# TensorE on zeros before the first keys, the second chunk's keys and queries loaded earlier, and the late relus, sums and stores rearranged, in a linear-attention and Fourier-mixing kernel

## The chip, the core and the metric

The kernel runs on one core of a Trainium2 chip. The core has five instruction queues that run side by side, each in its own program order, and wait for each other by semaphores: TensorE (matrix products; PE in the profile, with its weight loads as PEld), VectorE (DVE), ScalarE (ACT), GpSimd (POOL) and SyncE (SP), which here only issues DMA transfers. The metric is the device time of one execution in microseconds, lower is better.

## What is computed

Two blocks in a row. The first is a linear attention with decay, in 64-row blocks; the second takes its output as `x`, mixes it by a Fourier transform over sequence and width, normalises, and applies a two-layer network.

```python
# attention, per block of 64 rows (B=4, H=8, S=768, D=64)
intra = einsum(einsum(qb, kb) * Dmask, vb)
inter = einsum(qb * lam_pow, kv_state)
out[:, :, sl] = intra + inter
kv_state = lam_block * kv_state + einsum(kb * rev_pow, vb)

# x is (4, 768, 512)
mixed = real(fft(fft(x, axis=1), axis=2))
u = x + mixed
un = (u - mean(u)) / sqrt(var(u) + 1e-6)
out = u + maximum(un @ w_ch1, 0) @ w_ch2       # 512 -> 2048 -> 512
```

## The kernel before

Everything is float32. A float32 product shows in the profile as two TensorE records, a transpose (a product with an identity) as one.

**Front end.** `attn(b)` runs over six chunks of 128 rows of batch `b`. `attn_in(b, c)` issues three loads on SP's queue, `k`, `q` and `v` of the chunk (line 303, 256 KB each, from a pool of two buffers a name), makes the decayed keys `kd` on GpSimd (310), transposes keys (314) and queries (319) on TensorE and copies them out on ScalarE as `kT` (316) and `qT` (321). `attn_out` makes the scores (338), multiplies them by the decay on VectorE into `sc` (343), updates the state (358; 360 copies it for the first chunk, 362 and 363 add to it later), forms the output (373, 379), copies it out on ScalarE as `oT` (382) and turns it (395). Beside the attention of batch 0, `weights()` brings in the weights: each piece is a 512 KB load `raw` on SP (214), two ScalarE steps (225, 228) and five VectorE steps (226, 230, 232, 234, 235), because the weights come as 64-bit floats and are put together as float32 on the chip. The decay tables come from `lam` by scans on VectorE (161, 168).

The planner is a tile scheduler: it gives each instruction a place in its engine's queue by due times, except where the code pins the program order (`tc.keep_in_program_order`). The generators' `yield` values only set how pieces of work are woven.

**Middle.** The Fourier mixing (`fft_ln`) and the first four groups of the network (`mlp`, lines 749 and 763) are woven with the attention of the later batches.

**Late part.** Eight groups of 256 rows, in four pairs, go through the network by a seven-product scheme (Strassen-Winograd: sums of quarter matrices, seven products for eight). `late()` runs `first_layer(0)` for the first pair, and then `second_layer` and `deep_pair` for the others, in which each product is again split in seven (`seven`, lines 1124 and 1198). Of each of these products the seven parts are read out of PSUM by ScalarE (a first part) or VectorE (the others; 1206 in the second layer).

In `first_layer` block `i` of eight makes seven products of four TensorE records each, all on line 1031, in three PSUM banks X, Y and Z. This document names a product by its two factors (the names given to `prod`):

- `begin(i)`: X = a11·b11, copied out by ScalarE (1052); Y = a12·b21, added on VectorE (1054) and put through the relu there (1055); `begin` runs up to three blocks ahead.
- then X += s2·t2, copied out as `a12` (ScalarE, 1069); Z = s3·t3; X += s1·t1, copied out as `a22` (ScalarE, 1072); `a22` += Z (VectorE, 1073) and its relu (1074).
- `finish(i)`, one block later: X += s4·b22, whose relu goes out as `a21` (ScalarE, 1041, tile `sv` in the profile); Z += a22·t4; `a12` += Z (VectorE, 1043) and its relu (VectorE, 1044); `s1` = a21 + a22 (1045) and `s3` = a11 − a21 (1046).

A product that adds to a bank cannot start until the copy out of that bank before it is done: s1·t1 of a block waits for the copy 1069, s4·b22 for the copy 1072, a22·t4 for the addition 1073. In the profile the tiles `a11`, `a12`, `a22` are `ha`, and `s1`, `s3` are `hs`. Meanwhile GpSimd makes the sums of the second layer's weights (`keep_sums`, lines 855 and 859), four operations of 128x512 for each of seven products.

`inputs(j)` builds the sums of a later pair's input; its first step is the subtraction on line 941, pinned in VectorE's program order, which needs the tile `ur` loaded on line 894.

`store` (734) writes the result: rows of the lower half of a batch by SP (736), those of the upper half by an indirect DMA from GpSimd (738), whose rows come from an index table. `out_low` and `out_high` are two views of the output that the scheduler takes to be disjoint; two writes to the same view wait for each other. The last pair stores two upper tiles and two lower ones, the lower ones in pieces.

Of the kernel before, what the change touches and what calls it, by code (L numbers as in the profile page):

```python
# [11 lines left out]
F32 = mybir.dt.float32  # L12
# [4 lines left out]
AF = mybir.ActivationFunctionType  # L17
ALU = mybir.AluOpType
# [59 lines left out]
def kernel(  # L78
# [10 lines left out]
    nc = tc.nc  # L89
    B, H, S, D = q.shape  # L90
    DM = H * D
    DFF = moe_w_ch1.shape[1]
    C = 128
# [6 lines left out]
    HM = DM // 2  # L100
# [15 lines left out]
    def front_pool(name, bufs):  # L116
        return front_end.enter_context(tc.tile_pool(name=name, bufs=bufs, side="left"))
# [4 lines left out]
    const = front_pool("const", 1)  # L122
    ld = front_pool("ld", 2)
# [16 lines left out]
    def new(pool, shape, tag, **kw):  # L140
        cnt[0] += 1
        return pool.tile(shape, F32, tag=tag, name=f"{tag}{cnt[0]}", **kw)

    def psum_a(shape):
        return new(pa, shape, "pa")

    def psum_m(shape):
        return new(pm, shape, "pm")

    lamb = const.tile([128, H], F32, name="lamb")
    nc.scalar.dma_start(lamb, lam.rearrange("(o h) -> o h", o=1).broadcast_to([128, H]))
    ident = const.tile([128, 128], F32, name="ident")
# [30 lines left out]
    def row_of(j, n=128):  # L186
        return bass.IndirectOffsetOnAxis(ap=ix[0:n, j:j + 1], axis=0)
# [9 lines left out]
    def load_tables(i):  # L197
        if i == 1:
            nc.sync.dma_start(cs, cn["cs"].ap())
            nc.sync.dma_start(ix, cn["ix"].ap())  # L200
        elif i == 2:
            nc.sync.dma_start(dt, cn["dt"].ap())
# [80 lines left out]
    def pair(t, hp):  # L283
        return t[:, 2 * hp:2 * hp + 2, :].rearrange("p a d -> p (a d)")
# [6 lines left out]
            head = attn_in(b, c + 1) if c < NC - 1 else attn_in(b + 1, 0) if b in LEADS else ()  # L291
            yield from attn_out(b, c, head)

    ins, oTs, eo = {}, {}, {}
    LEADS = (0,)
    TURNED = (0,)
    first = const.tile([128, HP, 1], F32, name="first")

    def attn_in(b, c):
        rows = slice(c * C, (c + 1) * C)  # L300
        kt, qt, vt = (new(ld, [C, H, D], nm) for nm in ("k", "q", "v"))
        for t, src in ((kt, k), (qt, q), (vt, v)):
            nc.sync.dma_start(t, src[b, :, rows, :].rearrange("h p d -> p h d"))
        if b == 0:
            load_tables(c)

        kd = None
        if c < NC - 1:
            kd = new(at, [C, H, D], "kd")
            nc.gpsimd.tensor_tensor(kd, kt, kpow, op=ALU.mult)  # L310

        ptk = psum_a([128, HP, C])
        for hp in range(HP):
            nc.tensor.transpose(ptk[:, hp, :], pair(kt, hp), ident)  # L314
        kT = new(at, [128, HP, C], "kT")
        nc.scalar.copy(kT, ptk)
        ptq = psum_a([128, HP, C])
        for hp in range(HP):
            nc.tensor.transpose(ptq[:, hp, :], pair(qt, hp), ident)  # L319
        qT = new(at, [128, HP, C], "qT")  # L320
        nc.scalar.copy(qT, ptq)  # L321
        qs = None
        if c > 0:
            qs = new(at, [128, HP, C], "qs")
            nc.vector.tensor_tensor(qs, ptq, qpow, op=ALU.mult)
        ins[b, c] = kT, qT, qs, kd, vt
        yield 1.2

    def attn_out(b, c, head):
        kT, qT, qs, kd, vt = ins.pop((b, c))  # L330
# [9 lines left out]
        for hi in range(2):  # L340
            t = new(at, [C, HP, C], "sc", bufs=3)
# [11 lines left out]
        if not last:  # L353
            pu = psum_a([128, HP, D])
            for hp in range(HP):
                for hi in range(2):
                    h = 2 * hp + hi
                    mm(pu[HD[hi], hp, :], lhsT=kd[:, h, :], rhs=vt[:, h, :], start=True, stop=True)  # L358
            if c == 0:
                nc.vector.tensor_copy(s_new, pu)  # L360
            else:
                nc.gpsimd.tensor_tensor(s_new, s_old, spow.broadcast_to([128, HP, D]), op=ALU.mult)
                grown = nc.vector.tensor_tensor(s_new, s_new, pu, op=ALU.add)
            if not padded:
                yield 0.9
# [11 lines left out]
        for hp in range(HP):  # L377
            for hi in (1, 0) if padded else (0, 1):
                mm(po[HD[hi], hp, :], lhsT=vt[:, 2 * hp + hi, :], rhs=sc[hi][:, hp, :],  # L379
                   start=(c == 0 and hp == 0), stop=(hp == HP - 1), skip_group_check=True)  # L380
# [78 lines left out]

    uts, utd, ud, held = {}, {}, {}, {}  # L460
    ys = [const.tile([128, 2 * NK], F32, name=f"ys{i}") for i in range(5)]
    odd = const.tile([128, HM], F32, name="bs")
    for t in ys + [odd]:
        nc.gpsimd.memset(t, 0.0)

    gather = nc.gpsimd.indirect_dma_start
# [261 lines left out]
    ORDER = [(b, g) for b in range(B) for g in (1, 2, 0)]  # L728
    PLAIN, LATE = ORDER[:4], ORDER[4:]

    out_low, out_high = dram_disjoint_views(out.rearrange("b s d -> (b s) d"), 2)

    def store(b, T, y, cols=slice(0, DM)):
        if T < HC:
            row = S * b + 128 * T
            nc.sync.dma_start(out_low[row:row + 128, cols], y[:, cols])
        else:
            nc.gpsimd.indirect_dma_start(out=out_high,
                                         out_offset=row_of(2 + HC * (b + 1) + T - HC),
                                         in_=y[:, :], in_offset=None)  # L740

# [67 lines left out]
    V = nc.vector  # L809
# [108 lines left out]
    def inputs(j):  # L918

        P, r = pairs[j], s2.u.pop(j)  # L920
        b11, b21, b12, b22 = r[:, 0, 0:2], r[:, 0, 2:4], r[:, 1, 0:2], r[:, 1, 2:4]

        def sx(shape):
            return new(s2.hp, shape, "sx", bufs=6)

        P.U = U = dict(b11=b11, b21=b21, b22=b22, t3=b12)
        if j < DEEP:
            U["t1"], U["t2"], U["t4"] = t1, t2, t4 = [sx([128, 2, G * 128]) for _ in range(3)]
            V.tensor_tensor(t1, b12, b11, op=SUB)
            yield 0.0  # L930
            V.tensor_tensor(t2, b22, t1, op=SUB)
            yield 0.0
            V.tensor_tensor(t4, b21, t2, op=SUB)
            yield 0.0
            V.tensor_tensor(b12, b22, b12, op=SUB)
            yield 0.0
            return


        B11, B12, B21, B22 = (r[:, :, k::2, m:m + 128] for k in range(2) for m in (0, 128))  # L940
        tc.keep_in_program_order(V.tensor_tensor(B12, B22, B12, op=SUB))
        yield 0.0
        t1 = U["t1"] = sx([128, 2, G * 128])
        V.tensor_tensor(t1, b12, b11, op=SUB)
        yield 0.0
        V.tensor_tensor(b12, b22, b12, op=SUB)
        yield 0.0
        T2, T1, T4 = [sx([128, 2, 2, 128]) for _ in range(3)]
        V.tensor_tensor(T2, B12, B11, op=ADD)
        yield 0.0  # L950
        V.tensor_tensor(T1, B22, T2, op=SUB)
        yield 0.0
        V.tensor_tensor(T4, B21, T2, op=SUB)
        yield 0.0
        P.T = {n: [t[:, h, k] for t in (T1, T2, T4)]
               for n, h, k in (("b11", 0, 0), ("b21", 0, 1), ("t3", 1, 0), ("b22", 1, 1))}
        t2, t4 = U["t2"], U["t4"] = [sx([128, 2, G * 128]) for _ in range(2)]
        V.tensor_tensor(t2, b22, t1, op=SUB)
        yield 0.0
        q2, q1, q4 = [new(s2.hp, [128, 3, 128], "sv", bufs=3) for _ in range(3)]  # L960
        for i, n in enumerate(("t2", "t1", "t4")):
            C11, C12, C21, C22 = (U[n][:, k, m:m + 128] for k in range(2) for m in (0, 128))
            if n == "t4":
                nc.gpsimd.tensor_tensor(t4, b21, t2, op=SUB)
                yield 0.0
            nc.gpsimd.tensor_tensor(q2[:, i], C12, C11, op=ADD)
            nc.gpsimd.tensor_tensor(q1[:, i], C22, q2[:, i], op=SUB)
            nc.gpsimd.tensor_tensor(q4[:, i], C21, q2[:, i], op=SUB)
            P.T[n] = [q1[:, i], q2[:, i], q4[:, i]]
            yield 0.0  # L970
# [53 lines left out]
    def first_layer(j):  # L1024

        P = pairs[j]
        h, U = P.h, P.U

        def prod(ps, a, b, i, first):
            for kt in range(2):  # L1030
                nc.tensor.matmul(ps, lhsT=s2.A[a][:, kt, 128 * i:128 * i + 128], rhs=U[b][:, kt, :],  # L1031
                                 start=(first and kt == 0), stop=(kt == 1), skip_group_check=True)

        def two(t):
            return t.rearrange("p (s k) -> p s k", s=G)

        def finish(i, X, Z):
            a11, a12, a22, s1, s3 = (h[n][:, :, i, :] for n in ("a11", "a12", "a22", "s1", "s3"))
            prod(X, "s4", "b22", i, False)
            a21 = new(s2.hp, [128, G, 128], "sv", bufs=3)  # L1040
            nc.scalar.activation(a21, two(X), AF.Relu)
            prod(Z, "a22", "t4", i, False)
            V.tensor_tensor(a12, two(Z), a12, op=ADD)
            V.tensor_scalar(a12, a12, 0.0, None, op0=ALU.max)
            V.tensor_tensor(s1, a21, a22, op=ADD)
            V.tensor_tensor(s3, a11, a21, op=SUB)

# [13 lines left out]
        for i in range(HF):  # L1061
            a12, a22 = (h[n][:, :, i, :] for n in ("a12", "a22"))
# [375 lines left out]
```

## Time and profile before

| | us |
|---|---|
| median of 3 runs | 777.26 (775.27 to 777.77) |
| the profiled execution | 773.78 |
| its span | 771.7 |
| TensorE busy (5784 records) | 752.6, 98% of the span |
| VectorE busy | 602.8, 78% |
| ScalarE busy | 231.1, 30% |
| GpSimd busy | 178.4, 23% |

The span runs from the first instruction to the last that the profiler sees. A timeline line gives start, duration, engine, line of the kernel, operation, output tile and inputs, shapes and count; in square brackets stands the time that the engine sat idle before it and what ended that. The profile shows a granted clock of 1.00 in every slice. TensorE starts its first product at 5.05 us; after that it is idle for some 14 us in all, of which 1.6 us lie in three waits after 100 us, and 4.8 us at the very end.

### The profile page before, as it was taken

The page shows a single profiled execution, that of the slowest core. Times are in us where ns is not written, and L with a number is a line of the kernel's source. Part 1 is how long each engine was busy: PE and PEld are TensorE (multiplying, and loading weights), DVE is VectorE, ACT ScalarE, POOL GpSimd, SP SyncE. Part 2 cuts the span into 40 slices and gives each one's busy share as a digit, 9 for nine tenths or more (in the row PEclk, how much of TensorE's full clock was granted, in tenths as well). Part 3 has the DMA queues.
Part 4 walks back from the last instruction along what each step waited for, and adds up shares of the span by engine and source line. Part 5 has one row for each costly group of instructions (what it writes and reads, how often), then busy time and mean ns, then how long its engine had stood idle before and what let it go on. Part 6 is the DMA issues. An engine that isn't in the chain of part 4 may idle for free.

```text
span 771.7 us, 15006 instructions
## 1 busy us (share of the span) xinstructions
PE 752.6 (98%) x5784; PEld 646.7 (84%) x5784; DVE 602.8 (78%) x1167; ACT 231.1 (30%) x532; POOL 178.4 (23%) x202
## 2 busy tenths in 40 slices
PE   6989999999999999999999999999999999999997
PEld 5777877777685967769747899999999999999997
DVE  6999998784936575336898999788986699758984
ACT  3755443435521221322101221034301341024310
POOL 3223330021111113220105941360015001230013
PEclk9999999999999999999999999999999999999999
DMA  9979732347943149731433465876545456455442
GB/s 240 274 161 250 195 125 86 106 96 181 246 117 94 45 82 270 176 97 35 113 65 124 150 218 164 273 234 202 180 124 178 125 186 182 127 175 180 144 141 70
DMA packets 154924, 120.22 MB, mean 156 GB/s; under 512 B 114286, under 2 KB 116974, under 8 KB 154854
## 3 DMA queue, kind: packets, MB, share of 16 engines
q1 hardware_dynamic: 147792, 100.51, 46.7%
q0 software_dynamic: 4032, 12.99, 4.7%
q10 hardware_dynamic: 3030, 5.78, 2.1%
q8 instruction: 46, 0.75, 0.4%
q14 instruction: 24, 0.20, 0.1%
HBM read 88.04 MB, written 31.20 MB: 155 GB/s over the span
## 4 chain that ended last, share of the span: by engine, by line
PE 88%; DVE 7%; DMA 2%; ACT 1%; issue 1%; POOL 0%; SPq 0%; DVEq 0%; ACTq 0%
PE p L1198 22%; PE p L1124 17%; PE pm L763 13%; PE pm L749 13%; PE p L1031 6%; PE pa L603 3%; PE pa L379 3%; PE pa L338 3%; PE pa L373 2%; PE pa L314 1%; PE pa L358 1%; PE pa L395 1%; DVE sc L343 1%; PE pa L763 1%; PE pa L319 1%
## 5 line engine op out<-in xcount | busy, mean ns | idle before, releaser
L749 PE MATMUL pm<-ut,w 128*128 128x256 f32 x512 | 118.3, 381 | 0.0
L763 PE MATMUL pm<-w,hr 128*128 128x512 f32 x240 | 108.7, 596 | 0.1
L749 PEld LDWEIGHTS pm<-ut,w 128*128 128x128 f32 x512 | 94.7, 190 | 14.4 <-issue 2.7
L763 PEld LDWEIGHTS pm<-w,hr 128*128 128x128 f32 x240 | 43.8, 190 | 45.5 <-issue 43.8
L1219 POOL TENSOR_TENSOR y<-y,u 128x512 f32<-128x512 f32 x12 | 19.9, 1661 | 186.8 <-DVE y L1228 155.5
L1198 PE MATMUL p<-tx,sx 128*128 128x128 f32 x400 | 52.7, 275 | 0.0
L1198 PEld LDWEIGHTS p<-tx,sx 128*128 128x128 f32 x400 | 48.6, 192 | 0.0
L1133 DVE TENSOR_TENSOR ha<-p,ha 128x512 f32<-128x512 f32 x60 | 40.1, 686 | 8.6 <-PE p L1124 8.6
L1204 ACT COPY y<-p 128x128 f32<-128x128 f32 x48 | 12.8, 266 | 103.6 <-PE p L1198 103.1
L310 POOL TENSOR_TENSOR kd<-k,decay 128x512 f32<-128x512 f32 x20 | 21.7, 1083 | 86.5 <-PE pa L358 50.1
L343 DVE TENSOR_TENSOR sc<-pa,decay 128x512 f32<-128x512 f32 x48 | 30.9, 683 | 11.7 <-PE pa L338 11.5
L1206 DVE TENSOR_TENSOR y<-p,y 128x128 f32<-128x128 f32 x92 | 25.6, 285 | 15.6 <-PE p L1198 9.1
L1198 PE MATMUL p<-w,ha 128*128 128x128 f32 x288 | 37.4, 275 | 0.0
L1133 DVE TENSOR_TENSOR hs<-p,hs 128x512 f32<-128x512 f32 x39 | 26.2, 685 | 12.4 <-PE p L1124 12.4
L338 PEld LDWEIGHTS pa<-qT,kT 64*128 64x128 f32 x384 | 25.1, 193 | 12.2 <-ACT qT L321 6.4
L1198 PEld LDWEIGHTS p<-w,ha 128*128 128x128 f32 x288 | 34.9, 192 | 0.1
L638 POOL TENSOR_SCALAR ve<-mv 128x2 f32<-128x2 f32 x12 | 6.2, 519 | 120.0 <-DVE mv L635 120.0
L757 ACT ACTIVATE hr<-pm 128x256 f32<-128x256 f32 x44 | 16.7, 382 | 57.6 <-PE pm L749 53.7
L1124 PE MATMUL p<-sx,tx 128*128 128x128 f32 x264 | 33.9, 275 | 0.0
L338 PE MATMUL pa<-qT,kT 64*128 64x128 f32 x384 | 30.1, 292 | 2.9 <-ACT qT L321 2.9
L1124 PEld LDWEIGHTS p<-sx,tx 128*128 128x128 f32 x264 | 31.7, 192 | 0.0
L379 PE MATMUL pa<-sc,v 128*64 128x128 f32 x384 | 28.9, 282 | 1.3 <-DVE sc L343 1.0
(274 smaller groups left out, 1748.4 us busy)
## 6 DMA issues: line engine op xcount, KB each, us to landing
tx<-td SPq DMA_DIRECT2D x84, 256.0 KB, 2.9
raw<-in_moe_w_ch_dram SPq DMA_DIRECT2D x32, 512.0 KB, 4.3
tx<-sd SPq DMA_DIRECT2D x63, 256.0 KB, 2.8
k<-in_k_dram SPq DMA_DIRECT2D x24, 256.0 KB, 3.7
q<-in_q_dram SPq DMA_DIRECT2D x24, 256.0 KB, 7.0
v<-in_v_dram SPq DMA_DIRECT2D x24, 256.0 KB, 5.7
td<-tx SPq DMA_DIRECT2D x21, 256.0 KB, 2.0
ud<-x SPq DMA_DIRECT2D x16, 256.0 KB, 3.1
```

Source lines behind the costliest of these rows:

```text
L310: nc.gpsimd.tensor_tensor(kd, kt, kpow, op=ALU.mult)
L338: mm(pss[hi][:, hp, :], lhsT=kT[HD[hi], hp, :], rhs=qT[HD[hi], hp, :], start=True, stop=True)
L343: nc.vector.tensor_tensor(t, pss[hi], decay[:, hi::2, :], op=ALU.mult)
L379: mm(po[HD[hi], hp, :], lhsT=vt[:, 2 * hp + hi, :], rhs=sc[hi][:, hp, :], start=(c == 0 and hp == 0), stop=(hp == HP - 1), skip_group_chec ...
L603: mm = nc.tensor.matmul(ps[:, n, :], lhsT=piece(a, i, n), rhs=cs[0:rows, a, i in (2, 3), n, :], start=(a == 0), stop=(a == 1))
L749: nc.tensor.matmul(ps, lhsT=w1[:, c, 128 * fc:128 * fc + 128], rhs=ut[:, c, :], start=(c == 0), stop=(c == KO - 1))
L763: return nc.tensor.matmul(ps, lhsT=hr[(fc - f0) // 4][:, fc % 4, 128 * i:128 * i + 128], rhs=w2[:, fc, :], start=(fc == f0), stop=(fc == f ...
L1031: nc.tensor.matmul(ps, lhsT=s2.A[a][:, kt, 128 * i:128 * i + 128], rhs=U[b][:, kt, :], start=(first and kt == 0), stop=(kt == 1), skip_gro ...
L1124: nc.tensor.matmul(ps[:, 128 * i:128 * i + 128], lhsT=ab[m][0][:, 128 * i:128 * i + 128], rhs=ab[m][1], start=(start and i == 0), stop=Tru ...
L1133: V.tensor_tensor(o, p, o, op=ADD)
L1198: nc.tensor.matmul(ps[:, 0:HM // 2], lhsT=ab[m][0][i], rhs=ab[m][1][:, i, :], start=(start and i == 0), stop=(i == HF // 2 - 1), skip_grou ...
L1206: V.tensor_tensor(o, ps[:, 0:HM // 2], o, op=ADD)
```

## The change

```diff
--- before.py
+++ after.py
@@ -150,6 +150,18 @@
+    odd = const.tile([128, HM], F32, name="bs")
+    nc.vector.memset(odd, 0.0)
+    nothing = psum_m([128, 128])
+
+    def keep_on(n):
+
+        for _ in range(n):
+            tc.keep_in_program_order(
+                nc.tensor.matmul(nothing, lhsT=odd[:, 0:128], rhs=odd[:, 0:128], start=True, stop=True))
+
+    keep_on(9)
+
     lamb = const.tile([128, H], F32, name="lamb")
@@ -291,16 +303,26 @@
-    ins, oTs, eo = {}, {}, {}
+    ins, oTs, eo, loaded = {}, {}, {}, {}
...
     def attn_in(b, c):
-        rows = slice(c * C, (c + 1) * C)
-        kt, qt, vt = (new(ld, [C, H, D], nm) for nm in ("k", "q", "v"))
-        for t, src in ((kt, k), (qt, q), (vt, v)):
-            nc.sync.dma_start(t, src[b, :, rows, :].rearrange("h p d -> p h d"))
+
+        def load(c, *which):
+            rows = slice(c * C, (c + 1) * C)
+            for nm, src in which:
+                t = loaded[nm, b, c] = new(ld, [C, H, D], nm)
+                nc.sync.dma_start(t, src[b, :, rows, :].rearrange("h p d -> p h d"))
+
+        turned = (("k", k), ("q", q))
+        if ("k", b, c) not in loaded:
+            load(c, *turned)
+        load(c, ("v", v))
+        if (b, c) == (0, 0):
+            load(1, *turned)
+        kt, qt, vt = (loaded.pop((nm, b, c)) for nm in ("k", "q", "v"))
@@ -358,6 +380,8 @@
             if c == 0:
                 nc.vector.tensor_copy(s_new, pu)
+                if b == 0:
+                    keep_on(4)
@@ -459,8 +483,7 @@
-    odd = const.tile([128, HM], F32, name="bs")
-    for t in ys + [odd]:
+    for t in ys:
         nc.gpsimd.memset(t, 0.0)
@@ -728,14 +751,16 @@
-    out_low, out_high = dram_disjoint_views(out.rearrange("b s d -> (b s) d"), 2)
+    out_low, *out_high = dram_disjoint_views(out.rearrange("b s d -> (b s) d"), 3)
+    uppers = [0]
...
         else:
-            nc.gpsimd.indirect_dma_start(out=out_high,
+            uppers[0] += 1
+            nc.gpsimd.indirect_dma_start(out=out_high[uppers[0] % 2],
@@ -938,6 +963,7 @@
+        yield 0.0
         tc.keep_in_program_order(V.tensor_tensor(B12, B22, B12, op=SUB))
@@ -1041,7 +1067,7 @@
             V.tensor_tensor(a12, two(Z), a12, op=ADD)
-            V.tensor_scalar(a12, a12, 0.0, None, op0=ALU.max)
+            nc.scalar.activation(a12, a12, AF.Relu)
             V.tensor_tensor(s1, a21, a22, op=ADD)
```

Five things, by their places:

- Nine products of a 128x128 tile of zeros stand at the head of TensorE's queue, and four more behind the state update of batch 0's first chunk (line 358). Their result is not used. The tile of zeros is `odd`, which was cleared by GpSimd (464) and is now cleared by VectorE as its first instruction.
- On SP's queue `k` and `q` of batch 0's second chunk go out ahead of the first weight piece `raw`, not behind it. `v` of that chunk and all later loads keep their order.
- The relu of `a12` in `first_layer` (line 1044) goes from VectorE to ScalarE.
- In `inputs` the first subtraction (941) comes one step later, so that on VectorE one read of the second layer (1206) goes ahead of it, for each of three pairs.
- The upper stores go by turns through two views, so that each waits for the last but one and not for the one before it.

In the built order of the two kernels nothing else differs but this: the transposes of the second chunk's keys (314) stand on TensorE behind all of the first chunk's 379 and not between them, and the copy of these keys (316) on ScalarE behind `oT` (382) and the first weight piece's 225 and 228.

## The prediction

> **What bounds the kernel now.** I read the page's busy times first, then the chain of waits, then TensorE's own waits, then timelines of the places that the change touches.
>
> ```profile
> PE 752.6 (98%) x5784; PEld 646.7 (84%) x5784; DVE 602.8 (78%) x1167; ACT 231.1 (30%) x532; POOL 178.4 (23%) x202
> PE 88%; DVE 7%; DMA 2%; ACT 1%; issue 1%; POOL 0%; SPq 0%; DVEq 0%; ACTq 0%
> ```
>
> TensorE is the bound. VectorE, ScalarE or a DMA can only cost or give what TensorE waits for them, and those waits are few: 5.1 us for the first keys, some 6 us spread over 15 to 100 us, 0.8 us in `first_layer`, 0.6 us near 499 us, and the tail. So no part can gain much, but a new wait in the late part is lost in full, since TensorE has no idle time behind it in which to catch up.
>
> ```profile
> 5.05 1.08 PE L314 MATMUL pa<-ident,k 128*128 128x128 f32 x4 [5.05 <-DMA k<-in_k_dram]
> 7.96 2.08 PE L338 MATMUL pa<-qT,kT 64*128 64x128 f32 x16 [0.68 <-ACT qT L321]
> 11.45 1.12 PE L314 MATMUL pa<-ident,k 128*128 128x128 f32 x4
> 14.05 0.66 PE L319 MATMUL pa<-ident,q 128*128 128x128 f32 x4
> ```
>
> The start of the timeline: four transposes take 1.08 and 1.12 us until 12.6 us and 0.66 from 14 us on, and the sixteen score records 2.08 us, against 1.16 at 21.48. TensorE runs at about half its speed until some 13 us, 8 us after it begins, though the page's granted clock reads 1.00 throughout.
>
> ```profile
> 424.57 1.13 PE L1031 MATMUL p<-sx,w 128*128 128x256 f32 x4 [0.76 <-DVE ha L1073]
> 430.06 0.38 ACT L1041 ACTIVATE sv<-p 128x256 f32<-128x256 f32 x1 [1.35 <-PE p L1031]
> 431.97 0.37 ACT L1069 COPY ha<-p 128x256 f32<-128x256 f32 x1 [1.52 <-PE p L1031]
> 432.02 0.41 DVE L1045 TENSOR_TENSOR hs<-sv,ha 128x256 f32<-128x256 f32 x1
> 432.36 1.48 DVE L1046 TENSOR_TENSOR hs<-ha,sv 128x256 f32<-128x256 f32 x1
> 432.63 1.03 PE L1031 MATMUL p<-sx,w1s 128*128 128x256 f32 x4
> 433.76 0.41 DVE L1043 TENSOR_TENSOR ha<-p,ha 128x256 f32<-128x256 f32 x1
> 434.21 0.91 DVE L1044 TENSOR_SCALAR ha<-ha 128x256 f32<-128x256 f32 x1
> ```
>
> `first_layer`: VectorE is full, with operations that take 1.48 and 0.91 us while GpSimd works beside it (0.42 and 0.29 for the same after 453.4 us, when GpSimd has done). Block 2's addition 1043 comes at 433.76, while ScalarE has copied block 3's `a12` (1069) at 431.97 and TensorE has gone on with block 3's s1·t1 at 432.63.
>
> **The relus, worked out.** Taken from VectorE: eight times 0.91 us, which TensorE felt as 0.76 us once. Given to ScalarE: eight relus of some 0.40 us (1041, the same size out of PSUM, takes 0.38). ScalarE is idle most of the time here, so the work is free; the wait is not. In the built order ScalarE's queue reads 1041 of block i, the new relu of block i, 1069 of block i+1, 1072 of block i+1. The relu waits for VectorE's 1043 of block i, and behind it queue the two copies that TensorE's next products wait for.
>
> From s4·b22 of block i (435.22 for block 3) to s1·t1 of block i+1 (438.67) TensorE needs 3.45 us. The new path over the same stretch: 1.11 until 1041 starts (436.33), 0.38 for it, then 1045 and 1046, 0.42 for 1043, 0.40 relu, 0.37 copy, four handovers of 0.05: 2.88 us and the two sums. The sums take 0.75 us with GpSimd idle, 1.74 as at 432.02 to 433.76, 2.65 as at 420.18 to 422.83. So s1·t1 comes 0.18, 1.17 or 2.08 us late in each block, at the three speeds.
>
> Block by block: the relus of blocks 0 and 1 stand ahead of 1072. Block 0's 1043 ends at 423.24, so the relu ends at 423.7, block 1's copy at 424.05 instead of 422.50, and s4·b22 starts then, not at 422.79. The old wait of 0.76 us behind it goes, and block 1 leaves 0.4 us late. Block 2: VectorE has shed two relus, but has to wait for 1041 of block 1, which now comes later, and 1043 of block 2 ends at about 434.2 as before; relu to 434.6, copy to 435.0, s1·t1 of block 3 at 435.05 instead of 432.63: 2.4 us late in all. Blocks 3 and 4, with GpSimd still at work: 1.17 each. Blocks 5 and 6, after it: 0.18 each. Together 2.4 + 2.3 + 0.4 = **+5.1 us**. Bounds: if VectorE keeps the 0.9 us it shed, block 3 is 1.5 late, and with free sums 0.18 for each of four more, 2.2; if every block to the fifth meets the slow sums, 2.4 + 3 x 2.08 + 0.2 = 8.8; and if the relu never gates, the old wait goes, -0.8. I take 5.1, since 1.74 is the pitch of four of the six blocks in GpSimd's time.
>
> **The front, worked out.** Added: a clear of 128x256 on VectorE (GpSimd's took 0.30 us), hidden in VectorE's 3.76 us wait for `lam`; the same taken from GpSimd, which waits 3.47 us for the decay anyway. Nine products are 18 records. Eight of the nearest records (1198, 128x128) take 1.06 us with 0.28 for one alone, so 0.11 each, some 0.20 at the slow rate (2.08 to 1.16): 3.6 us, from 1.1 to about 4.8, when the first keys are still landing. A slower rate would push the transposes of 5.05 by 0.2 at most. The four later products, 0.9 us at full rate, stand between 358 and 379, where TensorE would wait for `sc`; at the slow rate they cost up to 1.6 us less that wait.
>
> When does the clock rise? Here it took 8 us from TensorE's first work, with gaps in it. Ends: up when the keys land at 5.05, or 8 us after the zeros begin, at 9.1. I take the middle, 7.0: queries transposed by 7.2, `qT` by 7.8, scores 7.85 to 9.0, `sc` at 9.05 instead of 10.07, state copied by 10.75. VectorE comes to the weight piece (226) next. That piece is late now: on SP's queue two loads, 512 KB, go ahead of it, and at the 250 GB/s of these microseconds that is 2 us; it landed about 8.6 (issued at 3.67, 4.9 to land) and now lands near 11. Behind it queue 226 (0.9), on ScalarE 228 (0.7), `oT` (0.6), 386 (0.2), 225 (0.7), then `kT` and `qT` of chunk 1 (1.2; `kT` was early before, but the scores need both): scores of chunk 1 at 15.3 instead of 15.91, their `sc` at 16.0 instead of 17.10. VectorE is full from there to 70 us and the chain of waits runs through it, so this carries on: **-1.0 us**. With the clock up only at 9.1 the same steps give -0.2. Bounds: -1.8 with the weight piece in time; +0.8 if the zeros do not raise the clock and the four later products run slow in front of 379.
>
> [...]
>
> **The rest.**
>
> ```profile
> 498.54 0.69 DVE L941 TENSOR_TENSOR ur<-ur 128x512 f32<-128x512 f32 x1 [2.70 <-DMA ur<-utd]
> 499.49 1.16 PE L1198 MATMUL p<-w2s,sx 128*128 128x128 f32 x8 [0.57 <-DVE y L1206]
> 765.63 0.97 POOL L738 DMA_INDIRECT out_dram<-y,ix  x1 [2.54 <-DVE y L1206]
> 766.90 0.29 DVE L1206 TENSOR_TENSOR y<-p,y 128x128 f32<-128x128 f32 x1 [0.60 <-PE p L1198]
> ```
>
> The sum 941 waits 2.70 us for its load with a read 1206 queued behind it, and TensorE waits 0.57 us for that read. With the read ahead of the sum this goes: **-0.6**, at worst 0; the other two pairs show no such wait. In the tail the second upper store had its last part from VectorE by 763.6 (a read at 763.32), but issued at 765.63: the first had gone at 762.11 and takes 2.9 to land, 765.0. DVE is named, but had long been done. Without that wait it issues near 763.9 and lands at 766.8. But VectorE's last read is at 766.90, the last SP store goes at 767.2 and lands 1.7 later, 768.9, while the old GpSimd store landed at 768.5: **-0.2**, between 0 and -0.4. The POOL waits of earlier pairs hide behind 50 us of its idle time.
>
> Sum: 5.1 - 1.0 - 0.6 - 0.2 = +3.3 us. The profiled execution took 773.78 (span 771.7 and 2.1 around it), so 777.1 by its clock; it lay 3.5 below the median of the runs, and I add to the median: 777.26 + 3.3 = **780.6 us**.
>
> **Rivals.** A difference under 0.3%, 2.3 us, can't be told from none: 774.9 to 779.6.
>
> Rival 1, the relu gates little: VectorE, rid of 0.9 us in each 5.58, catches up, the sums run at 0.75, and 2.2 us remain of the 5.1. Then 2.2 - 1.8 = +0.4, 777.7. For it: VectorE already gains on TensorE (5.58 against 6.05 us a block). Against it: in the new path VectorE waits for 1041 in every block, and being free earlier is of no use to it. Chance 0.24.
>
> Rival 2, faster: ScalarE's queue never stands in front of a product, the 0.76 wait goes, the front gains its 1.8, the sum 0.6 and the tail 0.4: -3.6, 773.7. It holds if 1043 of block i ends 2.6 us after s4·b22 starts (3.45 less relu, copy and handovers); the path there is 1.49, 0.75 for free sums, 0.42 and handovers, 2.76. Chance 0.12, for a ScalarE queue that is served otherwise than its order says, or sums shorter than any row here.
>
> Rival 3, the zeros don't do what they say (no rise of the clock): +0.8 instead of -1.0, 782.4. For it, 8 us of real work were needed; against it, nothing tells zeros from data in the rows. Chance 0.06; the forecast has 0.58.
>
> The forecast's own range is 777.5 to 785. The range given goes from 776.2 (the relus at 2.2, the rest at its best, -1.8 - 0.6 - 0.4, is 776.7; 0.5 more towards rival 2, which stays out) to 784.9 (the relus at 8.8, front and tail as taken, the 0.6 not got). 0.05 of the forecast's chance lies below 779.6, so: slower 0.58 - 0.05 + 0.06 = 0.59, same 0.24 + 0.05 = 0.29, faster 0.12.
>
> **What would show it.** In the changed profile: TensorE busy from about 1.1 us, the first query transposes near 0.66 us, and `sc` at about 8.9; in `first_layer` ScalarE's new relu idle before it on VectorE's addition, the copy of `a12` starting right behind it, and TensorE idle before s1·t1 "<- ACT ha" in blocks 3 to 5, with 3 to 7 us idle between 414 and 462; no wait near 499; the second upper store under 0.5 us after its read. I am wrong if TensorE's idle time in `first_layer` stays under 1.5 us, or if the relus end before s2·t2 does.

## The result, and the profile after

The changed kernel takes 781.84 us (median of 6 runs, 781.2 to 785.44), the kernel before 775.98 us (6 runs, 775.27 to 777.77) on the same chip: ratio 1.0081, 95% interval 1.0058 to 1.0105. A second group of runs gave 1.0067 (1.0046 to 1.0088). The change is slower, by 5 to 6 us; the prediction was 780.6. The profiled execution of the changed kernel took 781.20 us, its span is 778.9.

First the busy times on the page of the changed kernel:

```profile
PE 757.3 (97%) x5810; PEld 650.7 (84%) x5810; DVE 595.0 (76%) x1160; ACT 233.4 (30%) x540; POOL 177.2 (23%) x201
```

VectorE is rid of 7.8 us of work, and the time is longer. TensorE's waits tell why (us in total, times, longest):

```profile
PE p L1057 <- ACT ha L1095: 5.9, 3, 3.0
```

This line was not there before: three products s1·t1 wait for the copy of `a12` on ScalarE (1095 here, 1069 before; 1057 is the product's line, 1031 before). The old waits of 0.76 us for 1073 and of 0.57 us near 499 us are gone. The timeline around the longest wait, all engines in order of time:

```profile
431.43 0.38 ACT L1067 ACTIVATE sv<-p 128x256 f32<-128x256 f32 x1 [0.94 <-PE p L1057]
...
432.98 1.48 DVE L1071 TENSOR_TENSOR hs<-sv,ha 128x256 f32<-128x256 f32 x1
...
434.39 1.48 DVE L1072 TENSOR_TENSOR hs<-ha,sv 128x256 f32<-128x256 f32 x1
...
435.79 0.41 DVE L1069 TENSOR_TENSOR ha<-p,ha 128x256 f32<-128x256 f32 x1
436.24 0.42 ACT L1070 ACTIVATE ha<-ha 128x256 f32<-128x256 f32 x1 [4.43 <-DVE ha L1069]
436.56 0.35 ACT L1095 COPY ha<-p 128x256 f32<-128x256 f32 x1
436.97 1.13 PE L1057 MATMUL p<-sx,w1s 128*128 128x256 f32 x4 [2.99 <-ACT ha L1095]
437.94 3.34 PE L1057 MATMUL p<-ur,w 128*128 128x256 f32 x8
```

Read it from the bottom up: TensorE stood 2.99 us for the copy 1095. ScalarE itself had been idle for 4.43 us: it was held by the relu 1070, which stands ahead of that copy in its queue, and the relu by VectorE's addition 1069, which came behind the two sums 1071 and 1072 of 1.48 us each. And after the wait eight records take 3.34 us, which take 1.89 elsewhere in this stage. The table by stretches of the changed kernel shows the second effect (stretch, its length, the busy times of the engines in the order of the page, and ahead of the last two columns the granted clock):

```profile
6.00:9.00 3.00, 1.86 (x17) 1.55 (x18) 3.00 (x8) 1.17 (x2) 1.08 (x1) 0.86 1.21 240
9.00:12.00 3.00, 3.00 (x32) 2.66 (x29) 2.50 (x5) 0.00 (x0) 1.07 (x2) 0.57 0.99 300
434.00:438.00 4.00, 1.03 (x5) 0.93 (x6) 2.21 (x3) 0.68 (x2) 3.84 (x4) 1.00 0.34 125
438.00:442.00 4.00, 4.00 (x13) 3.22 (x12) 1.60 (x4) 0.74 (x2) 3.84 (x4) 0.57 0.41 152
```

The granted clock is halved for 3.41 us twice, each time behind a stretch in which TensorE worked only part of the time: 1.86 us in the 3 us of the first row, 1.03 in the 4 us of the third.

The timeline of TensorE in the front of the changed kernel:

```profile
1.18 3.95 PE L161 MATMUL pm<-bs 128*128 128x128 f32 x18 [1.18 <-DVE bs L154]
5.44 0.63 PE L336 MATMUL pa<-ident,k 128*128 128x128 f32 x4 [0.31 <-DMA k<-in_k_dram]
7.87 1.87 PE L360 MATMUL pa<-qT,kT 64*128 64x128 f32 x16 [0.68 <-ACT qT L343]
15.58 1.16 PE L360 MATMUL pa<-qT,kT 64*128 64x128 f32 x16 [0.84 <-ACT qT L343]
```

In this execution the clock is up before the keys come (transposes 0.63 us instead of 1.08), and the second chunk's scores start at 15.58 us, 15.91 before. Executions of one and the same front differ by more than that, as the experiments below show. The tail, GpSimd's second upper store and VectorE's last read:

```profile
772.88 0.98 POOL L763 DMA_INDIRECT out_dram<-y,ix  x1 [0.80 <-DVE y L1232]
...
775.88 0.29 DVE L1232 TENSOR_TENSOR y<-p,y 128x128 f32<-128x128 f32 x1 [0.60 <-PE p L1224]
```

The store starts 0.3 us after its last read has ended (772.31 and 0.29 us long), and from VectorE's last read to the end of the span there are 3.0 us, 4.8 before.

How far each instruction of `first_layer` lies behind its place in the profile of before: at 415 us 1.78 us, at 457.67 us (the first record of the second layer) 9.82. So this stage alone lost 8.0 us (8.1 in the second execution that was profiled), of which the forecast had 5.1.

### The profile page after: what moved, and what is told of

Read it like the earlier page. It is cut to its first block, busy times and chain, and to the rows that moved or that the text cites. A ratio compares the mean times of both kernels' runs of the same rounds, so it can differ in the third digit from the quotient of the medians.

```text
span 778.9 us, 15067 instructions
## 1 busy us (share of the span) xinstructions
PE 757.3 (97%) x5810; PEld 650.7 (84%) x5810; DVE 595.0 (76%) x1160; ACT 233.4 (30%) x540; POOL 177.2 (23%) x201
## 4 chain that ended last, share of the span: by engine, by line
PE 86%; DVE 8%; DMA 2%; ACT 2%; issue 1%; SPq 0%; POOL 0%; ACTq 0%; DVEq 0%
PE p L1224 22%; PE p L1150 17%; PE pm L788 13%; PE pm L774 13%; PE p L1057 4%; PE pa L626 3%; PE pa L360 3%; PE pa L403 2%; PE pa L397 2%; PE pa L380 1%; PE pa L419 1%; DMA raw<-in_moe_w_ch_dram 1%; DVE hs L1072 1%; PE pa L336 1%; PE pa L788 1%
## 5 line engine op out<-in xcount | busy, mean ns | idle before, releaser
L788 PEld LDWEIGHTS pm<-w,hr 128*128 128x128 f32 x240 | 43.8, 190 | 45.5 <-issue 43.8
L240 ACT ACTIVATE e<-e,cvt 128x512 uint16<-128x512 uint16 x32 | 23.2, 724 | 21.5 <-DVE e L238 21.4
```

The source lines that it names most:

```text
L240: nc.scalar.activation(pw, pw, AF.Relu, bias=cvt[:, 0:1], scale=8.0)
L788: return nc.tensor.matmul(ps, lhsT=hr[(fc - f0) // 4][:, fc % 4, 128 * i:128 * i + 128], rhs=w2[:, fc, :], start=(fc == f0), stop=(fc == f ...
```

## The experiments

Each kernel was timed beside the kernel before on one chip, in three groups; the ratio is to the kernel before of that group (medians 776.96, 775.18 and 775.98 us).

**The relu back on VectorE.** The changed kernel but for one line:

```diff
-            nc.scalar.activation(a12, a12, AF.Relu)
+            V.tensor_scalar(a12, a12, 0.0, None, op0=ALU.max)
```

> The changed kernel with the relu of a12 in first_layer on VectorE again; front, sum and stores stay changed. Theory (the relu on ScalarE costs the 7.8 us that TensorE loses between the products of 424 and 457 us in the changed kernel's trace): TensorE's waits for the copy of a12 go, the time is 781.8 - 7.8 = 774.0 us, ratio to the kernel before about 0.997, and in the profile the stretch of first_layer is as long as before. Rival (the late part only passes on what the front loses): 779 us or more. With the prediction's own 5.1 us it would be 776.7.

773.9 us, ratio 0.9957 (0.9938 to 0.9975). TensorE's only wait listed in `first_layer` is 0.41 us for 1099 (1073 before), and the stage loses 0.1 us against the profile of before:

```profile
437.58 1.13 PE L1057 MATMUL p<-sx,w 128*128 128x256 f32 x4 [0.41 <-DVE ha L1099]
```

The relu is what makes the change slow, and the rest of the change is a gain of 3.1 us.

**The relu alone.** The kernel before with the opposite line.

> The kernel before with nothing but the relu of a12 on ScalarE. Theory: 776 + 7.8 = 783.8 us, ratio about 1.010, the same three waits of TensorE for the copy of a12 (3.0, 1.2, 1.7 us) and one window of about 3.4 us at half the granted clock behind the longest. The prediction's size: 776 + 5.1 = 781.1. Rival (the relu costs only together with the changed front, which lets blocks meet GpSimd's sums differently): under 779.

784.44 us, ratio 1.0075 (1.0045 to 1.0105). The stage loses 6.4 us. The wait shows in other portions than in the changed kernel, and no half-clock stretch follows:

```profile
427.77 1.13 PE L1031 MATMUL p<-ur,w1s 128*128 128x256 f32 x4 [1.04 <-ACT ha L1072]
...
438.62 1.13 PE L1031 MATMUL p<-sx,w1s 128*128 128x256 f32 x4 [1.81 <-ACT ha L1069]
439.58 1.89 PE L1031 MATMUL p<-ur,w 128*128 128x256 f32 x8
...
446.57 1.13 PE L1031 MATMUL p<-sx,w1s 128*128 128x256 f32 x4 [1.65 <-ACT ha L1069]
```

The relu costs without the changed front too. My expectation of a half-clock stretch missed: with the longest wait at 1.81 us the eight records behind it take 1.89.

**The relu on ScalarE, but behind the copies.** The changed kernel with the relu issued later, pinned in ScalarE's order; `held` carries `a12` from `finish` to the next block, and the last block's relu follows its `finish`:

```diff
             V.tensor_tensor(a12, two(Z), a12, op=ADD)
-            nc.scalar.activation(a12, a12, AF.Relu)
+            held.append(a12)
...
-            nc.scalar.copy(a22, two(X))
+            tc.keep_in_program_order(nc.scalar.copy(a22, two(X)))
+            while held:
+                relu(held.pop())
```

> The changed kernel with the relu of a12 still on ScalarE, but placed behind the next block's copy of a22 in ScalarE's queue, so that neither copy which TensorE waits for stands behind a relu that waits for VectorE. Theory (its place in the queue costs, not the engine): TensorE's waits for the copy of a12 go, 773.5 to 775 us. Rival (a relu on ScalarE costs wherever it stands, by its 0.42 us of service or since a later user of a12 waits): 779 us or more.

772.68 us, ratio 0.9944 (0.9923 to 0.9965): faster than both kernels. ScalarE's timeline of it:

```profile
431.44 0.37 ACT L1100 COPY ha<-p 128x256 f32<-128x256 f32 x1 [1.34 <-PE p L1057]
433.17 0.37 ACT L1103 COPY ha<-p 128x256 f32<-128x256 f32 x1 [1.35 <-PE p L1057]
433.44 0.42 ACT L1087 ACTIVATE ha<-ha 128x256 f32<-128x256 f32 x1
```

Both copies (1100 of `a12`, 1103 of `a22`) now start on TensorE's word, and the relu (1087) has its input ready when its turn comes. TensorE has no wait at all in `first_layer`. So the place in the queue costs, not the engine.

**The same on the kernel before**, with front, sum and stores unchanged.

> The kernel before with the relu of a12 on ScalarE behind the next block's copy of a22; front, sum and stores as before. Theory: no wait of TensorE in first_layer, also not the 0.76 us of before, so 0.5 to 1 us less than before, ratio 0.9988. If the ScalarE relu costs there, ratio over 1.002.

773.98 us, ratio 0.9974 (0.9955 to 0.9992). TensorE has no wait in `first_layer`, and its distance to the profile of before falls from 1.47 to 0.33 us over the stage, 1.1 us; the interval reaches from 0.6 to 3.5 us of gain.

**Zeros in the longest wait.** The changed kernel with four products of a 64-column zero tile (`none`) added to Z of block 3, ahead of the s1·t1 that waited:

```diff
             prod(Z, "s3", "t3", i, True)
+            if i == 3:
+                for _ in range(4):
+                    tc.keep_in_program_order(
+                        nc.tensor.matmul(Z[0:64], lhsT=none, rhs=U["t3"][:, 0, :], start=False, stop=True, skip_group_check=True))
```

> The changed kernel with four products of a 64-column tile of zeros added to bank Z of block 3 of first_layer, in front of the s1*t1 that waited 2.99 us for the copy of a12 (some 1.9 us of TensorE work that ends before the copy). Theory (the idle stretch lets the granted clock fall to half for 3.41 us, and this makes eight records of 1.89 us take 3.34 to 3.42): no half-clock stretch between 430 and 450 us, these records 1.9 us, 1.4 to 1.6 us less than the changed kernel: 780 us, ratio 1.005 to 1.006. Rival (the records slow down for another cause, or the waits behind only grow by as much): same as the changed kernel, ratio 1.007 to 1.008.

779.26 us, ratio 1.0033 (1.0019 to 1.0048), and in TensorE's timeline:

```profile
433.76 1.94 PE L1102 MATMUL p<-ur,none 128*64 128x256 f32 x8
436.82 1.13 PE L1059 MATMUL p<-sx,w1s 128*128 128x256 f32 x4 [1.12 <-ACT ha L1097]
437.79 1.89 PE L1059 MATMUL p<-ur,w 128*128 128x256 f32 x8
```

The product still cannot start before 436.8, but the eight records behind it are back at 1.89 us, and the stage loses 6.8 us instead of 8.0. The half clock had cost 1.7 us (1.45 on these eight records and 0.28 on the four behind them); 0.4 of it comes back, since the next block's wait grows from 1.24 to 1.66 us. By the ratios the kernel is 0.34% or 0.48% faster than the changed kernel in its two measurements, 2.6 or 3.7 us; these were taken in other groups, and the difference is too uncertain to say more than its sign. One profile shows the clock at 1.00 from 430 to 450 us, and the runs agree: the mean granted clock (one such fall takes 0.002 off it) is at most 0.998 in all 15 runs of the changed kernel, and 0.999 or 1.000 in five of the twelve runs here. So the idle stretch is what halved the clock.

**The front: zeros alone, loads alone.** The kernel before with the first and the fourth piece of the diff, and with its second piece alone.

> The kernel before with the zeros alone (nine products at the head, four behind the first state update); loads, relu, sum and stores as before. The front as a whole is worth 0.9957 / 0.9993 = 0.9964, some 2.8 us, by the first group of runs. Theory (the zeros carry it, by an earlier full clock): ratio 0.996 to 0.998, second chunk's scores 0.7 us or more earlier than in before. Rival (the loads carry it): within 0.1% of before.

> The kernel before with only the keys and queries of the second chunk ahead of the first weight piece. The engines' orders but SP's are those of before. Theory (zeros carry the front): within 0.1% of before or slower, up to +1 us, since the weight piece lands some 2 us later and VectorE's weight work waits for it. Rival (the loads carry the front, since later keys and weight pieces then come in a better order): ratio 0.996 to 0.998. If neither of the two alone shows it, it takes both.

Zeros 774.77 us, 0.9981 (0.996 to 1.0002); loads 774.22 us, 0.9978 (0.996 to 0.9995). Neither alone carries the front: each half seems to be worth about 1.5 us, though the first interval touches one. With the zeros alone the second chunk's scores start at 13.65 us, 2.3 us earlier than in the profile of before:

```profile
13.65 1.16 PE L350 MATMUL pa<-qT,kT 64*128 64x128 f32 x16 [0.83 <-ACT qT L333]
```

In the six profiles that have zeros and loads they start at 14.30 to 15.58 us. In five of them VectorE's first step on the weight piece waits 0.4 to 1.2 us for its load; with the zeros alone it does not. In the second profile of the changed kernel:

```profile
11.48 0.43 DVE L238 TENSOR_SCALAR e<-raw 128x512 uint16<-128x512 uint16 x1 [1.13 <-DMA raw<-in_moe_w_ch_dram]
```

So at this point, as far as one profile with the zeros alone can show, the loads take back part of what the zeros give. Single profiles say little on what is left of it later, since executions of one and the same front differ by more. A row of TensorE shows this, the turning of `oT` at 66 us. In the kernel before and, with the same front, in the kernel with the relu alone:

```profile
65.94 0.66 PE L395 MATMUL pa<-ident,oT 128*128 128x128 f32 x4 [0.82 <-ACT oT L382]
```

```profile
68.99 0.66 PE L395 MATMUL pa<-ident,oT 128*128 128x128 f32 x4 [1.01 <-ACT oT L382]
```

The same row in all profiles, in the order before, relu alone, sum and stores, stores alone, sum alone, relu behind on the kernel before; and changed kernel, the same again, relu back, relu behind, five more zeros, zeros in the longest wait:

| front | start of the row, us | mean |
|---|---|---|
| as before | 65.94, 68.99, 69.39, 68.69, 68.65, 67.90 | 68.3 |
| changed | 67.09, 66.53, 67.15, 66.00, 68.55, 67.38 | 67.1 |
| zeros alone | 68.06 | |
| loads alone | 67.79 | |

The profile of before happened to be some 3 us early here, about the 3.2 us between its time of 773.78 and the median of the first group (776.96). Read against that one profile, the changed front seems to lose 1.2 us. By the means of six and six it gains 1.1 us, and at the start of `first_layer` (its first row of four records) 1.0; the scatter leaves about 1.5 us either way.

**The stores and the sum**, together and apart, on the kernel before.

> The kernel before with the upper stores by turns through two views and the sum behind one read; relu and front as before. Theory by the two traces: the 0.57 us wait near 499 us goes and the stretch from VectorE's last read to the end of the span shrinks from 4.8 to 3.1 us: -0.6 - 1.8 = -2.4 us, ratio 0.997. The prediction's sizes give -0.8 us, ratio 0.999. Rival (the shorter tail of the changed kernel comes from its other parts): tail 4.6 us or more.

> The kernel before with the upper stores by turns through two views, and nothing else. Theory by four traces: VectorE's last read to the end of the span 3.1 us instead of 4.8, -1.7 us, ratio 0.998. The prediction's 0.2 us: ratio 1.000.

> The kernel before with the sum of inputs behind one read, and nothing else. Theory (the wait near 499 us goes, but two products later TensorE waits 0.43 and 0.15 us for reads, as in the kernel with sum and stores): 0 to -0.2 us, ratio 1.000. The prediction: -0.6 us, ratio 0.9992; the times can't tell these apart, the waits in the trace can.

Together 776.43 us, 0.9993 (0.9976 to 1.0011); the stores alone 774.8 us, 0.9978 (0.9966 to 0.9989); the sum alone 776.69 us, 1.0001 (0.9985 to 1.0016). GpSimd's timeline with the stores alone:

```profile
764.74 0.98 POOL L740 DMA_INDIRECT out_dram<-y,ix  x1 [5.49 <-DVE y L1208]
766.52 0.97 POOL L740 DMA_INDIRECT out_dram<-y,ix  x1 [0.80 <-DVE y L1208]
```

The second store waits 0.80 us instead of 2.54, and from the last read (769.53) to the end of the span (772.7) there are 3.2 us. This stretch is 3.0 to 3.4 us in all eight profiles with the stores by turns and 4.7 to 4.9 in all six without: the stores are worth 1.7 us. With the sum moved too, TensorE waits again a little later (timeline of the kernel with both):

```profile
502.24 1.06 PE L1201 MATMUL p<-w2s,sx 128*128 128x128 f32 x8
...
505.52 1.16 PE L1201 MATMUL p<-tx,sx 128*128 128x128 f32 x8 [0.43 <-DVE y L1209]
...
507.72 1.16 PE L1201 MATMUL p<-tx,ha 128*128 128x128 f32 x8 [0.15 <-DVE y L1209]
```

The product that waited 0.57 us for a read starts at once, but two later ones now wait 0.43 and 0.15 us for theirs: VectorE's sum has to be done somewhere, and a read stands behind it there. With the sum alone no such wait is listed, so the expected two did not come, but TensorE's records stand further apart at the same place. More profiles settle what is left. From the second layer's first record to the first of `deep_pair` TensorE takes 43.7 to 44.5 us in the six profiles with the old order and 42.9 to 43.2 in the eight with the new one; in the stretch behind it, up to the next pair's second layer, 43.8 us in all six, and 43.8 to 44.9 in the eight. Over both together the mean falls from 87.8 to 87.3 us: about 0.5 us is gained, and how much of the freed time is lost again differs from execution to execution. Together, stores and sum should give at least what the stores give alone; they gave 0.5 us, with an interval that reaches from a gain of 1.9 us to a loss of 0.9, so this is not settled beyond that.

**The changed kernel again, and five more products of zeros.** The second of these is the kernel with the relu behind the copies and zeros between the first transposes and the scores:

```diff
             nc.tensor.transpose(ptk[:, hp, :], pair(kt, hp), ident)
+        if (b, c) == (0, 0):
+            keep_on(2)
...
             nc.tensor.transpose(ptq[:, hp, :], pair(qt, hp), ident)
+        if (b, c) == (0, 0):
+            keep_on(3)
```

> The changed kernel itself, once more beside the others of this group. If its loss is as measured, ratio 1.008 (782 to 783 us) and TensorE waits of 5 to 6 us for the copy of a12; and since three profiles have put the stretch to 66 us 3.05 to 3.45 us (old front, two kernels) or 1.2 us and less (new front, three kernels) behind the profile of before, its scores of the second half of the front should again lie nearer to the profile of before than the old front's do.

> The kernel with the relu behind the copies (772.7 us in the first group), and five more products of zeros in TensorE's waits between the transposes of the first chunk and its scores, two behind the keys and three behind the queries. Theory (the clock falls behind a stretch in which TensorE does little but transposes, and this costs the front up to 1 us in some executions): no half-clock stretch between 6 and 15 us, 0 to 1 us faster than 772.7. Rival (loads and VectorE set the front, a faster TensorE there gains nothing, and the zeros delay qT's users): 772.5 to 774.

The changed kernel: 781.36 us, the 1.0067 named above. TensorE waits 6.0 us for the copy of `a12`, and `oT` is turned at 66.53 us, both as expected. In this execution the clock did not fall at 8 us, but it did in `first_layer`. The zeros between: 771.99 us, 0.9942 (0.9921 to 0.9964), against 0.9944 without them: no difference that can be seen. The clock, once up, stays up until 15 us (transposes of 0.60 to 0.66 us from 5.04 us on), but so it did in five of the six other profiles with zeros at the head, so the trial says little on whether these zeros are needed; at 28 us it falls here too, for 3.41 us (four transposes at 28.64 us take 1.06).

## Why the prediction was right, and where its sum was not

**The relus.** Right in direction, cause and place: ScalarE's queue, the relu behind VectorE's addition, the copy of `a12` behind the relu, TensorE idle in blocks 3 to 5 (2.99, 1.24 and 1.69 us), and gone when the relu stands behind the copies. The term of 5.1 us was too small in two ways. The step "I take 5.1, since 1.74 is the pitch of four of the six blocks" failed: in the kernel with the relu alone block 1 leaves 0.4 us late and block 3 2.2 in all, as worked out (0.4 and 2.4), but blocks 4 and 5 add 1.9 and 2.0 each, not 1.17, since their two sums take 2.55 and 2.63 us, close to the upper bound of 2.65. In block 3 only the second sum is slow (0.41 and 1.48 us), in blocks 4 and 5 both are (1.22 and 1.48, 1.30 and 1.48). In the profile of before the sums of two SBUF tiles (1045, 1046) take up to 1.49 us while GpSimd makes its own sums and 0.42 behind them, the additions from PSUM (1043) 0.41 and 0.42, and the relus on VectorE, with one input in SBUF, mostly 0.91 and 0.29. Why the first and the last are slowed and the additions not, no run here shows. The other part was not in the sum at all: the half clock behind the longest wait, which costs 1.7 us where it falls and 1.2 us of the stage. So the term is 6.4 to 6.8 without it and 8.0 with it.

**The front.** Predicted -1.0 within -1.8 to +0.8. It was not measured closely. The kernel with the relu back and the kernel with sum and stores alone differ in the front only: 0.9957 to 0.9993, -2.8 us, but with intervals of about 1.4 us on each this reaches from -0.8 to -4.8. The kernel with the relu back against the one with the stores alone gives -1.6, with the sum's share still in it, and the rows of twelve profiles -1.0 to -1.1. So the predicted size is not refuted. That the zeros raise the clock held: by the lengths of its records TensorE reaches full speed 4.1 to 7.3 us into the span in seven profiles with zeros at the head and 10.9 to 14.0 in seven without. The prediction took 7.0, the middle of two ends that it read from the rows; the seven lie between 2.9 us before that and 0.3 behind it. That the late weight piece gives part of it back is seen at the second chunk's scores (13.65 us against 14.30 to 15.58). What the prediction had not foreseen is that the loads alone, which delay that piece, gained as much as the zeros alone; what their 1.7 us (interval 0.4 to 3.1) consist of was not found.

**The sum.** Predicted -0.6. The wait near 499 us went, as said. Part of it came back behind it, between nothing and 1.1 us; the step named only the read that was freed, not the reads that would stand behind the sum next. On average over the profiles 0.5 us stayed, near the forecast; the times alone (1.0001, 0.9985 to 1.0016) cannot tell this from nothing.

**The stores.** Predicted -0.2 within 0 to -0.4, measured -1.7. The failed step is that the last SP store, landing at 768.9, sets the end. The span ended at 771.7, and 2.8 us were left unexplained there; a store issued 1.7 us earlier on GpSimd moved that end by 1.7 us, so the end hung on the indirect store. Why the span goes on for some 3 us past that store's landing no row shows.

**The sum of it.** By stages of the profiles the parts are 8.0 - 1.0 - 0.5 - 1.7 = +4.8 us; measured were +5.2 and +6.3 in two groups, with intervals of 1.6 and 1.8 us either way. The three gains make 3.2 us, and the kernel with the relu back gained 3.1. So the sum closes within the noise. The forecast rise was 3.3 us. It was short by 2.9 on the relus and long by 1.5 on the stores, and these partly cancel, which is luck. So is some of the agreement of the times, 780.6 and 781.84 us: the 777.26 that the rise was added to came from three runs, and six gave 775.98.

**The rivals.** "The relu gates little" falls by the three waits; "the zeros don't raise the clock" by the seven profiles. Of "faster", the tail came true, even larger than it had it; only the relu's place kept the change from it, as the kernel with the relu behind the copies shows.

## What to carry to other kernels

Before a cheap operation goes to an idle engine, write down what stands behind it in that engine's queue: here ScalarE stood 4.43 us ahead of a relu of 0.42 us that waited for VectorE, TensorE stood 2.99 us for the copy behind that relu, and the stage lost 8.0 us, with ScalarE busy for only 30% of the span. Put it behind the instructions that the bound engine waits for, and pin it there if a scheduler orders the queue. And compare a new trace with more than one trace of the old kernel: here the profiled execution of the kernel before lay 3.2 us below the median of its group (773.78 against 776.96 us), and turned `oT` at 65.94 us, where the other five with its front did at 67.90 to 69.39.

## What was not expected of the hardware

A wait of 3.0 us cost more than itself. In both profiles of the changed kernel the granted clock fell to 0.50 for 3.41 us behind it, 1.7 us of lost work, while behind waits of 1.81 and 1.65 us in the kernel with the relu alone it did not, and 1.94 us of zeros in the same place kept it up. TensorE did not stand still throughout: in the second execution it worked 1.02 of the 4 us ahead of it, and at 6 to 9 us in the first, around the other fall, 1.86 of 3 us. Falls of the same length stand in five other profiles, at 27 to 29 us (sum alone, loads alone, sum and stores, five more zeros) and at 69 us (zeros in the longest wait), each behind 4 us in which TensorE worked 0.7 to 2.4 us. Whether a given execution is hit depends on more than the kernel: of two profiles of the changed kernel one shows the fall at 8 us, the other not.
